# A state update in column tiles of 32 instead of 64, with every engine's order listed anew

## The chip, the cores and the metric

The kernel runs on one core of a Trainium2 chip. The time is the device time of one execution in microseconds (us). The core's engines are TensorE (PE in the rows; PEld is its weight load), VectorE (DVE), ScalarE (ACT), GpSimd (POOL) and SyncE (SP), which issues the DMAs.

## The reference

For 4 batches, 8 heads, 768 steps and 48 features there is a linear recurrence with a complex decay, and behind it a gated layer with a convolution of three taps over the steps:

```python
mag = np.sqrt(a_re * a_re + a_im * a_im)
scale = np.minimum(mag, 0.999) / (mag + 1e-06)
a_re_n, a_im_n = (a_re * scale, a_im * scale)
for t in range(S):
    ar, ai = (a_re_n[:, :, t, :, None], a_im_n[:, :, t, :, None])
    new_re = ar * S_re - ai * S_im
    new_im = ar * S_im + ai * S_re
    kv = np.einsum('bhd,bhe->bhde', k[:, :, t], v[:, :, t])
    S_re, S_im = (new_re + kv, new_im)
    y[:, :, t] = np.einsum('bhd,bhde->bhe', q[:, :, t], S_re)
...
h = np.maximum(x @ w_in, 0.0)          # x: heads side by side, 384 wide; h: 1024 wide
conv_out += conv_w[k][None, None, :] * hp[:, k:k + S, :]
gate = 1.0 / (1.0 + np.exp(-conv_out))
return (h * gate @ w_out)
```

## The kernel before

The steps are cut into chunks of 128, six to a batch, 24 in all, and into 12 segments of two chunks. A segment's decays are turned into running logarithms and angles (`a_pre`, `a_log`, `a_trig`, `c_pre`), then into factors for q and k (`c_exp`, `c_post`); VectorE and ScalarE do this. L553 multiplies k (then q) by the factors into `qkc`, L557 writes that to DRAM (`qk_d`), and L559 reads it back in another layout as `stk`, with 96 rows per head (48 features, real and imaginary).

For a chunk, `c_chunk` turns the 6 blocks of k back to steps by features (transposes, L572), copies them out as `kn` (L573, ScalarE), and adds k times v to a state that stays in PSUM: this is the state update, L579. L586 copies the state to `s_sb`. Then `attention` computes the scores of the chunk (L612, column tiles of 64, 96 rows), masks them (L627), and adds to one PSUM tile, by L636, state by query ("state-by-query", 128 moving columns) and p by v ("p v", 64 moving columns), both in column tiles of 32. `in_turn` writes these so that the four column tiles follow one another: a matmul of tile 0, one of tile 1, of tile 2, of tile 3, and round again. L662 and L663 split the result into two parts for the layer behind.

The layer runs in 10 units of 256 or 384 steps. `moe_front` (L718) multiplies by `w_in`, then relu (L722) and the convolution (L723, L725); `moe_back` has the gate (L413, L737, L743, L746), the product with `w_out` (L753), and the output (L760, L763). These matmuls use the whole array. Weights are unpacked at the start by VectorE, ScalarE and TensorE (L338 to L341, L376 to L383).

The state has 96 rows per head and `kn` 96 columns. Before the change L579 covers them by two column tiles of 64: rows 0 to 63 and 64 to 127. The second takes 32 columns of the next head along (for the last head, 96 columns of zeros that L322 sets once). So one chunk has 8 heads x 2 = 16 matmuls of 64 weight columns and 48 moving columns. An f32 matmul has two records in the trace here (two passes), so a chunk shows 32. Five chunks of a batch's six have an update: 20 in all, 640 records.

The order on each engine is written out by hand. `groups` numbers the program's instructions as they are written (matmuls that follow one another with the same operand and job share a number), `ORDER` lists the numbers for each engine, and `in_order` ties each instruction to the one listed ahead of it:

```python
for eng, line in ORDER.items():
    ...
            for i in row:
                if last is not None:
                    tc.add_manual_dep(i, last.name, ...)
                last = i
```

In the old list the 20 updates have the numbers 178, 184, 240, 246, 389, 595, 601, 767, 773, 961, 1103, 1109, 1240, 1246, 1435, 1577, 1583, 1714, 1720 and 1894. The constants of the convolution are the numbers 36 (its DMA, L346) and 37 to 46 (VectorE, L338 to L357); 19 is the first segment's load of a (L443), 20 its square (L458), 21 the sum behind that (L459), 22 its logarithm (L413).

Of the kernel before, what the change touches and what calls it, by code (L numbers as in the profile page):

```python
# [12 lines left out]
F32 = mybir.dt.float32  # L13
# [7 lines left out]
B, H, S, D = 4, 8, 768, 48  # L21
# [25 lines left out]
QC = 2  # L47
TB = 3
# [21 lines left out]
DSEG = [0] * 12  # L70
# [89 lines left out]
    "DVE": [37, 38, 39, 40, 21, 41, 112, 42, 48, 113, 43, 49, 56, 46, 50, 64, 45, 114, 24, 27, 25, 57, 28, 29, 30,  # L160
# [113 lines left out]
def linear_attention_moe_kernel(ctx: ExitStack, tc: tile.TileContext, a, qk, v, w_in, conv_w, w_out, out):  # L274
    nc = tc.nc

    const = ctx.enter_context(tc.tile_pool(name="const", bufs=1))
# [117 lines left out]
    st = {}  # L395
# [144 lines left out]
    def c_post(p):  # L540
        seg_time(p, OP)
        b, j, m = segs[p]
# [22 lines left out]
    def c_chunk(c, kv, stk, vt):  # L565
        b, j = divmod(c, NC)
        if j < NC - 1:
# [6 lines left out]
            if j == 0:  # L574
                st["sps", b] = psS.tile([128, H, D], F32, name="s_ps")
# [460 lines left out]
```

## Time and profile before

| | |
|---|---|
| median of 3 runs | 393.89 us (392.82 to 394.5) |
| the profiled execution | 393.71 us |
| its span, first to last instruction | 391.9 us |
| mean granted TensorE clock | 0.971 |
| TensorE, VectorE, ScalarE busy | 340.1, 346.8, 336.0 us |

The time of an execution holds a little more than the span (1.8 us here). Busy time is the union of an engine's instructions; a matmul's row also holds the time that it takes to pass through the array, so matmuls overlap, and what a matmul occupies is read from one start to the next.

### The profile page before, as it was taken

The page shows a single profiled execution, that of the slowest core. Times are in us where ns is not written, and L with a number is a line of the kernel's source. Part 1 is how long each engine was busy: PE and PEld are TensorE (multiplying, and loading weights), DVE is VectorE, ACT ScalarE, POOL GpSimd, SP SyncE. Part 2 cuts the span into 40 slices and gives each one's busy share as a digit, 9 for nine tenths or more (in the row PEclk, how much of TensorE's full clock was granted, in tenths as well). Part 3 has the DMA queues.
Part 4 walks back from the last instruction along what each step waited for, and adds up shares of the span by engine and source line. Part 5 has one row for each costly group of instructions (what it writes and reads, how often), then busy time and mean ns, then how long its engine had stood idle before and what let it go on. Part 6 is the DMA issues. An engine that isn't in the chain of part 4 may idle for free.

```text
span 391.9 us, 11311 instructions
## 1 busy us (share of the span) xinstructions
PE 340.1 (87%) x4834; PEld 318.4 (81%) x4834; DVE 346.8 (89%) x567; ACT 336.0 (86%) x555; POOL 5.7 (1%) x38
## 2 busy tenths in 40 slices
PE   0307178899999999999999999999997999999993
PEld 0105147799999998999999999999996999999992
DVE  3999999999999999899999989999998877569680
ACT  5999999999999999899999999999996965354561
POOL 4000000000000000000000000000000000000000
PEclk9999666999999999999999999999999999999999
DMA  7999979895986648794947937939939529101011
GB/s 279 339 336 325 279 256 299 302 243 174 298 236 264 182 104 288 245 267 164 263 170 246 257 110 286 244 96 343 264 129 263 200 82 252 33 22 44 0 42 51
DMA packets 33420, 81.07 MB, mean 207 GB/s; under 512 B 2128, under 2 KB 23632, under 8 KB 31824
## 3 DMA queue, kind: packets, MB, share of 16 engines
q1 hardware_dynamic: 33360, 80.25, 65.2%
q8 instruction: 40, 0.66, 0.7%
q14 instruction: 20, 0.16, 0.1%
HBM read 56.65 MB, written 23.59 MB: 205 GB/s over the span
## 4 chain that ended last, share of the span: by engine, by line
PE 78%; ACT 12%; DVE 6%; issue 2%; DMA 1%; DVEq 0%; ACTq 0%
PE h_ps L718 27%; PE o L753 27%; PE ps L636 9%; PE ps L612 8%; PE s_ps L579 4%; PE ps L572 3%; ACT L265 3%; ACT w_t L458 1%; ACT x_t L413 1%; DVE qkc_t L553 1%; ACT w_t L413 1%; DMA a_t<-in_a 1%; ACT e_t L413 1%; ACT zz_t L413 1%; ACT wi L376 1%
## 5 line engine op out<-in xcount | busy, mean ns | idle before, releaser
L718 PE MATMUL h_ps<-x,wi 128*128 128x258 f32 (+1 forms) x720 | 121.0, 307 | 0.0
L753 PE MATMUL o<-wo,hg 128*128 128x384 f32 x576 | 120.6, 341 | 0.1
L718 PEld LDWEIGHTS h_ps<-x,wi 128*128 128x128 f32 x720 | 109.2, 189 | 1.0 <-ACT h_t L722 0.2
L753 PEld LDWEIGHTS o<-wo,hg 128*128 128x128 f32 x576 | 98.5, 188 | 2.2 <-issue 0.5
L265 ACT ACT_TABLE_LOAD x45 | 57.7, 1283 | 0.8
L612 PE MATMUL ps<-stk 96*64 96x128 f32 (+1 forms) x768 | 41.7, 260 | 8.8 <-DMA stk<-qkd 8.3
L413 ACT ACTIVATE g_t<-g_t,cw 128x256 f32<-128x256 f32 (+1 forms) x80 | 42.1, 547 | 8.0 <-DVE g_t L725 7.5
L612 PEld LDWEIGHTS ps<-stk 96*64 96x64 f32 x768 | 37.1, 144 | 14.0 <-ACT zz_t L525 8.5
L723 DVE SCALAR_TENSOR_TENSOR g_t<-h_t,cw 128x256 f32<-128x256 f32 (+1 forms) x80 | 41.3, 532 | 4.6 <-ACT h_t L722 4.3
L722 ACT ACTIVATE h_t<-h_ps 128x258 f32<-128x258 f32 (+1 forms) x80 | 33.2, 424 | 13.8 <-PE h_ps L718 13.7
L553 DVE TENSOR_TENSOR qkc_t<-e_t,zz_t 128x1536 f32<-128x1536 f32 x24 | 41.9, 1751 | 0.5 <-ACT zz_t L413 0.5
L725 DVE SCALAR_TENSOR_TENSOR g_t<-h_t,cw,g_t 128x256 f32<-128x256 f32 (+1 forms) x80 | 41.3, 533 | 0.8
L737 DVE SCALAR_TENSOR_TENSOR g_t<-g_t,h_t 128x512 f32<-128x512 f32 (+1 forms) x40 | 31.6, 792 | 5.3 <-ACT g_t L413 5.3
L746 DVE TENSOR_TENSOR hg<-g_t,hg 128x512 fp32r<-128x512 f32 (+1 forms) x40 | 31.5, 792 | 4.8 <-ACT hg L743 4.7
L743 ACT ACTIVATE hg<-g_t 128x512 fp32r<-128x512 f32 (+1 forms) x40 | 28.6, 715 | 8.1 <-DVE g_t L737 5.0
L627 DVE TENSOR_TENSOR p_t<-ps,mask 128x384 f32<-128x384 f32 x48 | 26.4, 552 | 5.8 <-PE ps L612 4.8
L636 PE MATMUL ps<-p_t,v_t 128*32 128x64 f32 x1344 | 24.6, 222 | 4.9 <-DVE p_t L627 2.5
L572 PE MATMUL ps<-ident,qkc_t 128*128 128x128 f32 x120 | 18.5, 289 | 11.5 <-DVE qkc_t L553 10.2
L636 PEld LDWEIGHTS ps<-p_t,v_t 128*32 128x32 f32 x1344 | 22.4, 112 | 6.4 <-issue 3.2
L572 PEld LDWEIGHTS ps<-ident,qkc_t 128*128 128x128 f32 x120 | 14.6, 148 | 14.2 <-DVE qkc_t L553 11.1
L579 PE MATMUL s_ps<-v_t,kn 128*64 128x48 f32 x640 | 24.0, 231 | 2.1 <-ACT kn L573 2.1
L579 PEld LDWEIGHTS s_ps<-v_t,kn 128*64 128x64 f32 x640 | 22.0, 147 | 4.6 <-ACT kn L573 3.6
(91 smaller groups left out, 446.1 us busy)
## 6 DMA issues: line engine op xcount, KB each, us to landing
qkd<-qkc_t SPq DMA_DIRECT2D x24, 768.0 KB, 4.0
stk<-qkd SPq DMA_DIRECT2D x24, 768.0 KB, 7.8
v_t<-in_v SPq DMA_DIRECT2D x12, 1024.0 KB, 7.8
a_t<-in_a SPq DMA_DIRECT2D x12, 768.0 KB, 5.3
qk_t<-in_qk SPq DMA_DIRECT2D x12, 768.0 KB, 5.8
out<-os_t SPq DMA_DIRECT2D x24, 192.0 KB, 3.0
hg<-in_w_out SPq DMA_DIRECT2D x8, 384.0 KB, 5.4
h_t<-in_w_in SPq DMA_DIRECT2D x8, 384.0 KB, 5.8
```

The lines of the kernel that those rows point to most:

```text
L265: row = [nc.scalar.preload_act_table_set(loaded).ins] + row
L413: nc.scalar.activation(out, in_, func=func, **kw)
L553: nc.vector.tensor_tensor(out=qkc, in0=e[:, q:q + 1].broadcast_to([128, 2, NG * w]), in1=zz, op=ALU.mult)
L572: nc.tensor.transpose(tr[:, g - lo], kv[:, g // NG, g % NG], ident)
L579: nc.tensor.matmul(sps[r:r + 64, h], lhsT=kn[:, h * 96 + r:h * 96 + r + 64], rhs=vt[:, j % 2, h // 2, 112 * (h % 2):112 * (h % 2) + D], st ...
L612: nc.tensor.matmul(o, lhsT=kt[:, 2 * i + u, part * HC + r:part * HC + r + TM], rhs=qt[:, 2 * i + u, part * HC:C], start=first, stop=part = ...
L636: nc.tensor.matmul(yp[r0:r0 + 32, q // 4, cols], lhsT=left, rhs=right, start=r0 not in started, stop=stop, tile_position=(0, r0), skip_gro ...
L718: nc.tensor.matmul(hp, lhsT=wi[iw][:, f, kt], rhs=x[ix][:, kt], start=(k == 0), stop=(k == 8))
L722: nc.scalar.activation(h, hp, func=AF.Relu)
L723: nc.vector.scalar_tensor_tensor(out=g, in0=h[:, 0:n], scalar=cw[:, f, 0:1], in1=h[:, 1:n + 1], op0=ALU.mult, op1=ALU.add)
L725: nc.vector.scalar_tensor_tensor(out=g, in0=h[:, 2:n + 2], scalar=cw[:, f, 2:3], in1=g, op0=ALU.mult, op1=ALU.add)
L753: nc.tensor.matmul(ops[t][:min(C, n - t * C)], lhsT=hg[:, k, t * C:min((t + 1) * C, n)], rhs=w[:, fw], start=(f == 0 and i == 0), stop=(f ...
```

## The change

The update goes back to three column tiles of 32 for each head: 8 x 3 = 24 matmuls of 32 weight columns per chunk, the three tiles in turn. `kn` has 8 x 96 columns again and comes from a pool with one buffer; its zero columns and their memset (number 17) are gone, so that all higher numbers of the list stand one lower. The state has 96 rows instead of 128. The write of `qkc` to DRAM is written as two runs of a row instead of one. `DSEG` gets longer. All five lists of the order are new; they hold the same groups as before, the memset left out.

```diff
+KB = 1
...
-DSEG = [0] * 12
+DSEG = [0] * 24
...
-    "PE": [52, 53, 60, 61, 174, 176, 178, 68, 69, 180, 76, 182, 77, 186, 188, 84, 92, 93, 85, 190, 195, 184, 197,
...
-    "DVE": [37, 38, 39, 40, 21, 41, 112, 42, 48, 113, 43, 49, 56, 46, 50, 64, 45, 114, 24, 27, 25, 57, 28, 29, 30,
...
-    "ACT": [20, 22, 23, 26, 115, 159, 34, 33, 51, 2, 59, 204, 54, 161, 206, 163, 31, 207, 210, 164, 166, 167, 121,
...
-    "SP": [19, 36, 111, 47, 55, 63, 165, 32, 203, 117, 123, 71, 79, 227, 216, 87, 129, 340, 169, 95, 135, 172, 170,
...
+    "PE": [51, 59, 52, 67, 68, 60, 75, 76, 173, 175, 179, 177, 181, 183, 185, 187, 83, 84, 189, 194, 91, 92, 196,
...
+    "DVE": [36, 37, 38, 39, 40, 41, 42, 43, 44, 111, 45, 112, 20, 47, 113, 48, 55, 49, 63, 56, 64, 26, 23, 24, 57,
...
+    "ACT": [2, 19, 21, 22, 114, 25, 158, 32, 58, 50, 33, 53, 203, 160, 66, 205, 30, 162, 206, 69, 209, 163, 165, 166,
...
+    "SP": [35, 18, 110, 46, 54, 62, 164, 31, 202, 116, 122, 70, 78, 226, 86, 215, 339, 128, 134, 168, 94, 171, 169,
...
-    kn = const.tile([128, (H + 1) * 96], F32, name="kn")
-    nc.gpsimd.memset(kn[:, H * 96:], 0.0)
...
-            nc.sync.dma_start(qk_d.rearrange("p g t -> p (g t)"), qkc.rearrange("p c x -> p (c x)"))
+            nc.sync.dma_start(qk_d.rearrange("p (c g) t -> p c (g t)", c=2), qkc)
...
-            knv = kn[:, 0:H * 96].rearrange("s (h d c) -> s (h d) c", h=H, c=6)
+            kn = sc.tile([128, H, 96], F32, name="kn", bufs=KB)
+            knv = kn.rearrange("s h (d c) -> s (h d) c", c=6)
...
-                st["sps", b] = psS.tile([128, H, D], F32, name="s_ps")
+                st["sps", b] = psS.tile([96, H, D], F32, name="s_ps")
...
-                for r in range(0, 128, 64):
-                    nc.tensor.matmul(sps[r:r + 64, h], lhsT=kn[:, h * 96 + r:h * 96 + r + 64],
+                for r in range(0, 96, 32):
+                    nc.tensor.matmul(sps[r:r + 32, h], lhsT=kn[:, h, r:r + 32],
...
-                           in_=sps[0:96].rearrange("r (i u) d -> r i u d", u=2))
+                           in_=sps.rearrange("r (i u) d -> r i u d", u=2))
```

Where the updates stand in TensorE's two lists, from the third p v on (the last 16 of the 20): in the old one five between two groups of scores, four between scores and L636, six between the layer's matmuls and transposes, one between scores and L718. In the new one six between scores and L636, three between L636 and scores, six between the layer's matmuls and transposes or other matmuls of the layer, one between L753 and scores. Counting every place behind the third p v where the width of the column tiles changes (32, 64 or the whole array), the old list has 79 and the new one, with the update at 32, has 80. The number of activation table loads that the order of ScalarE asks for is 45 by either list.

## Rows read from the trace of the kernel before

**Rows 1.** The page's first part: the span and the engines' busy time.

```profile
span 391.9 us, 11311 instructions
PE 340.1 (87%) x4834; PEld 318.4 (81%) x4834; DVE 346.8 (89%) x567; ACT 336.0 (86%) x555; POOL 5.7 (1%) x38
```

**Rows 2.** The chain that ended last, by engine and by line.

```profile
PE 78%; ACT 12%; DVE 6%; issue 2%; DMA 1%; DVEq 0%; ACTq 0%
PE h_ps L718 27%; PE o L753 27%; PE ps L636 9%; PE ps L612 8%; PE s_ps L579 4%; PE ps L572 3%; ACT L265 3%; ACT w_t L458 1%; ACT x_t L413 1%; DVE qkc_t L553 1%; ACT w_t L413 1%; DMA a_t<-in_a 1%; ACT e_t L413 1%; ACT zz_t L413 1%; ACT wi L376 1%
```

**Rows 3.** Busy time by stretch (PE, PEld, DVE, ACT, POOL; clock, DMA share, GB/s).

```profile
30.00:50.00 20.00, 9.92 (x77) 7.90 (x79) 20.00 (x39) 19.80 (x28) 0.00 (x0) 0.80 0.99 301
50.00:75.00 25.00, 19.64 (x324) 15.14 (x322) 24.93 (x35) 24.85 (x37) 0.00 (x0) 0.75 0.89 274
75.00:120.00 45.00, 44.61 (x748) 42.68 (x744) 44.45 (x77) 43.43 (x87) 0.34 (x4) 1.00 0.80 240
...
346.50:385.40 38.90, 38.87 (x357) 38.23 (x355) 27.79 (x62) 21.07 (x50) 0.00 (x0) 1.00 0.09 32
```

**Rows 4.** The same from 75 us to the last update: sum of five stretches.

```profile
sum 271.50, PE 267.78 PEld 255.48 DVE 250.32 ACT 244.04 POOL 1.37; mean PE 53.56 PEld 51.10 DVE 50.06 ACT 48.81 POOL 0.27
```

**Rows 5.** Groups of instructions, shapes apart.

```profile
L636 PE MATMUL ps<-p_t,v_t 128*32 128x64 f32 x1344 | 24.6, 222 | 4.9 <-DVE p_t L627 2.5 <-issue 2.4
L579 PE MATMUL s_ps<-v_t,kn 128*64 128x48 f32 x640 | 24.0, 231 | 2.1 <-ACT kn L573 2.1
L636 PE MATMUL ps<-stk,s_sb 96*32 96x128 f32 x640 | 22.8, 283 | 0.8 <-issue 0.6
```

**Rows 6.** Busy time of L579 alone, 75 us to the last update.

```profile
75.00:346.50 271.50, 17.83 (x512) 16.32 (x512) 1.00 0.69 211
```

**Rows 7.** Timeline of TensorE around one update (start, length, group, records).

```profile
93.30 0.89 PE L612 MATMUL ps<-stk 96*64 96x128 f32 x16
94.04 1.14 PE L579 MATMUL s_ps<-v_t,kn 128*64 128x48 f32 x32
95.00 0.85 PE L612 MATMUL ps<-stk 96*64 96x128 f32 x16
95.79 1.08 PE L636 MATMUL ps<-stk,s_sb 96*32 96x128 f32 x32
```

**Rows 8.** Timeline of TensorE: an update ahead of transposes, and a p v.

```profile
117.30 1.14 PE L579 MATMUL s_ps<-v_t,kn 128*64 128x48 f32 x32
118.37 0.77 PE L572 MATMUL ps<-ident,qkc_t 128*128 128x128 f32 x5
...
138.74 0.97 PE L636 MATMUL ps<-p_t,v_t 128*32 128x64 f32 x56
139.63 0.45 PE L753 MATMUL o<-wo,hg 128*128 128x384 f32 x1
```

**Rows 9.** TensorE's waits from 75 to 358 us (total, times, longest).

```profile
PE ps L636 <- issue: 3.0, 2, 2.4
```

**Rows 10.** Timeline of VectorE and ScalarE at the start.

```profile
5.44 0.18 DVE L338 TENSOR_SCALAR ct<-cd 128x24 int32<-128x24 int32 x1 [5.44 <-DMA cd<-in_conv_w]
5.66 0.18 DVE L339 SCALAR_TENSOR_TENSOR ct<-cd,ct 128x24 int32<-128x24 int32 x1
...
6.77 0.96 DVE L459 CUSTOM_DVE_ANT_0 w_t<-w_t 128x768 f32<-128x768 f32 x1 [0.51 <-ACT w_t L458]
...
5.26 1.48 ACT L458 ACTIVATE w_t<-a_t 128x1536 f32<-128x1536 f32 x1 [3.17 <-DMA a_t<-in_a]
8.05 1.48 ACT L413 ACTIVATE w_t<-w_t 128x1536 f32<-128x1536 f32 x1
```

**Rows 11.** DMA packets of the whole run, and two kinds of issue.

```profile
DMA packets 33420, 81.07 MB, mean 207 GB/s; under 512 B 2128, under 2 KB 23632, under 8 KB 31824
qkd<-qkc_t SPq DMA_DIRECT2D x24, 768.0 KB, 4.0
v_t<-in_v SPq DMA_DIRECT2D x12, 1024.0 KB, 7.8
```

More of the change, by code (lines that the diff above doesn't have):

```diff
@@ L105 @@
 ORDER = {
[54 rows of a table removed]
-    "DVE": [37, 38, 39, 40, 21, 41, 112, 42, 48, 113, 43, 49, 56, 46, 50, 64, 45, 114, 24, 27, 25, 57, 28, 29, 30,
[27 rows of a table removed]
-    "ACT": [20, 22, 23, 26, 115, 159, 34, 33, 51, 2, 59, 204, 54, 161, 206, 163, 31, 207, 210, 164, 166, 167, 121,
[25 rows of a table removed]
-    "POOL": [191, 3, 192, 10, 4, 15, 18, 11, 5, 13, 0, 8, 1, 9, 12, 16, 14, 7, 6, 17, 398, 397, 609, 608, 790, 789,
[8 rows of a table removed]
[54 rows of a table added]
+    "DVE": [36, 37, 38, 39, 40, 41, 42, 43, 44, 111, 45, 112, 20, 47, 113, 48, 55, 49, 63, 56, 64, 26, 23, 24, 57,
[27 rows of a table added]
+    "ACT": [2, 19, 21, 22, 114, 25, 158, 32, 58, 50, 33, 53, 203, 160, 66, 205, 30, 162, 206, 69, 209, 163, 165, 166,
[25 rows of a table added]
+    "POOL": [190, 3, 191, 10, 4, 15, 17, 11, 5, 13, 0, 8, 1, 9, 12, 16, 14, 7, 6, 397, 396, 608, 607, 789, 788, 1116,
[8 rows of a table added]
 }
```

224 rows, old and new, of the table ORDER are left out of this document.

## The prediction

> **What bounds the kernel now.** I read the chain of waits first: 78% of the time that ends last is TensorE's, and the state update L579 has 4% of it [rows 2]. That VectorE has more busy time than TensorE over the run [rows 1] misleads, since the stretches differ. Up to 75 us VectorE and ScalarE are full and TensorE is not; from 75 us on TensorE is full, to its last matmul at 385.4 us [rows 3]; behind that come only the last output and its DMA, to the span's end at 391.9 [rows 1]. So an update behind the third p v (16 of the 20) counts in full on the path that sets the end, and the four ahead of it are covered by VectorE's and ScalarE's work: there the same microsecond buys nothing. From 75 us to the last update TensorE is busy 267.78 of 271.5 us, VectorE 250.32, ScalarE 244.04 [rows 4]: the next engine has 17 us less to do than TensorE, so a few us off TensorE do not make another engine the bound over the whole stretch, though between 75 and 120 us VectorE has only 0.55 us to spare [rows 3].
>
> **The update itself.** What a group occupies is read from starts. In a group, records follow one another at (its length - one record's own length) / (records - 1). The update has 32 records in 1.14 us, one lasting 0.231 us: 0.909 / 31 = 29.3 ns each, so 59 ns for two neighbours, one on each column tile [rows 7, 5]. Over the 16 updates it is 17.83 / 16 = 1.114 us a group, 28.5 ns a record, and 32 x 28.5 = 0.91 us occupied [rows 6].
>
> The trace of before has no update in tiles of 32. The nearest rows are L636's, which has tiles of 32 in turn. The p v has 56 records in 0.97 us, one lasting 0.222 us: 13.6 ns each, 55 ns for a round of four tiles, at 64 moving columns [rows 8, 5]. State by query has 32 records in 1.08 us, one lasting 0.283 us: 25.7 ns each, 103 ns a round, at 128 columns [rows 7, 5]. So a round of tiles of 32 is set by the moving columns, at (103 - 55) / 64 = 0.75 ns a column, and at 48 columns it should take 55 - 16 x 0.75 = 43 ns. Is there a floor that keeps it at 55? For tiles of 64 there is one: the scores' 16 records occupy 0.74 us from their start to the update's [rows 7], half of them with 128 columns (4 pairs at about 0.103) and half with 64, which leaves 0.33 for 4 pairs and for the change of tile width at their head, at most 0.08 a pair; the update, with a quarter fewer columns, still takes 0.059. There the columns seem to count no longer, and something of the tile's width does. With half the width, whatever it is should be half: the four tiles' weight loads fit into 55 ns, so three take no more than 41. Both ways say about 42. I take 43: per chunk 8 heads x 2 passes = 16 rounds, 16 x 43 = 0.69 us in place of 0.91, 0.22 us less, and 16 x 0.22 = 3.5 us over the run. Bounds: with no round shorter than the shortest seen, 55 ns, it is 0.88 and the gain 16 x 0.03 = 0.5 us; with 0.75 ns x 48 = 36 ns and nothing else it is 0.58 and the gain 5.3 us.
>
> **Changes of tile width.** An update ahead of scores (64 and 64) holds TensorE 0.96 us until the next start, one ahead of transposes (64 and whole) 1.07 us [rows 7, 8]: 0.11 us for the change. From p v to L753 it is 0.89 us where 0.76 are records: 0.13 us. With tiles of 32 the update no longer fits between scores: the five updates that stand so in the old list would make ten changes of 0.12 us, 1.2 us. The new list moves them next to L636, and in sum 79 changes become 80: +0.1 us. Bounds 0 and +0.5 (a change into narrow tiles may cost more than one out of them).
>
> The Trainium skill states the rule behind this (TensorEngine Tiling, Key Properties): changing the tiling mode drains the array. Rule and rows agree here; by it alone, with the old positions kept, the 3.5 us would shrink by the 1.2 us worked out above.
>
> **Issue.** TensorE gets 256 records and as many weight loads more behind the third p v. In 75 to 358 us it stood still twice, 3.0 us in sum, for nothing but "issue", both times in L636's dense bursts [rows 9], which are nearly all of L636's 1,984 records [rows 5]. At that rate 256 more records bring 256 / 1,984 x 3.0 = +0.4 us; bounds 0 and one more stall of the longest sort, +2.4.
>
> **The start.** In the new list of VectorE the sum L459 is no longer fifth but stands behind all ten operations for the convolution's constants and two for the weights, and the constants' DMA is issued ahead of the load of a. Ten operations at 0.22 us from start to start and two longer ones of the weights (about 0.3 and 0.5 us on the engine), some 2.9 us, from 5.44 us on put L459 at 8.3 instead of 6.77, or a little earlier as its constants arrive earlier; the logarithm L413, at 8.05 now, needs its result [rows 10], 0.9 us later, so some 9.0 to 9.2. That is up to 1.1 us of ScalarE idle at the head of a stretch in which ScalarE is full (19.80 of 20.00) [rows 3]. VectorE loses nothing, the twelve had to be done anyway. I take half, +0.5; bounds 0 and +1.1.
>
> **What costs nothing.** The memset is one short instruction on GpSimd, which is idle 99% of the time and busy 5.7 us in 38 instructions [rows 1], 0.15 us each; without that cover so much would be gained. The write of `qkc` in two runs: the load of v is written in two runs too, and above 8 KB there are 33,420 - 31,824 = 1,596 packets, which are its 12 x 128 and little else [rows 11]: runs that adjoin go as one packet. If not, 24 x 128 more packets of half the size, same bytes, behind a landing of 4.0 us. `kn` from a pool of one buffer waits for the update before it, as the one tile did. L586 reads 96 rows either way. `DSEG` is read for 12 segments. Activation tables: 45 loads by both lists.
>
> **The rest of the new order.** The groups are the same, so each engine's sum is the same. Adding up, each instruction at its duration in the old trace (whose sums are [rows 1]), the work that is listed ahead of each of the 24 splits L663, VectorE's differs by at most 1.5 us between the lists for 23 of them; TensorE's ahead of each L636 by at most 2.3. A local reshuffle, with no stall of its own in sight: 0, bounds -1.5 and +3 (TensorE's 3.0 us of waits [rows 9] once more).
>
> **Sum**, against the profiled 393.71 us: -3.5 + 0.1 + 0.4 + 0.5 = -2.5, 391.2 us. The profiled execution is 0.18 us below the median of the runs, so I predict 391.4.
>
> **Rivals.**
> 1. A price per record. If an update's record costs the same whatever its width, 48 x 28.5 = 1.37 us a chunk, 0.46 more, 16 x 0.46 = +7.4, with the other +1.0 some 402 us. For it: in tiles of 64, moving columns no longer count. Against: 13.6 ns a record in the p v, with the same 128 rows and 32 columns [rows 8]. It decides for slower from (0.91 + 0.06) / 48 = 20 ns a record, with the other terms as above. Chance 0.08.
> The Trainium skill has a rule of that kind (TensorEngine Tiling, Instruction Overhead: about 60 cycles a matmul, so that no tiles should be taken from a dimension already small). By its figure, as an estimate, 25 ns x 48 = 1.2 us a chunk and 4.5 us in all, near 399 us; the 13.6 ns speak against it.
> 2. No round below 55 ns: gain 0.5 us, with the other +1.0 a time of 394.4, same. For it: no shorter round is in the trace. Chance 0.13.
> 3. The gain on TensorE comes true and goes into its waits for VectorE and ScalarE, full as those are up to 75 us, VectorE nearly so up to 120 [rows 3]: 393 to 395. Against it: 17 us to spare in sum [rows 4]. Chance 0.17.
> 4. The new lists cost by themselves: a group that TensorE reaches 2 to 5 us ahead of its data, so that all matmuls behind it wait. In the new list one L663, that of the 22nd chunk, has 4.9 us more of VectorE's work ahead of it, and transposes need the bank that it frees. With the start: 396 to 399. Chance 0.10.
> 5. The new lists gain as well, in the start or in the waits: 387 to 389. Chance 0.06.
>
> **How the numbers follow.** The forecast holds 0.46; its own range is 389 to 392.5, from the bounds of the sum. What a measurement here can tell from no change is 0.5%, 2 us: 391.9 and 395.9. Of the forecast 0.02 falls into "same". Faster 0.44 + 0.06 = 0.50; same 0.13 + 0.17 + 0.02 = 0.32; slower 0.08 + 0.10 = 0.18. The range reaches down to the bound of the update's gain with a little of case 5 (387.5) and up to the end of "same" (396), which leaves out case 1, most of case 4 and half of case 5, 0.2 together.
>
> **What would show it.** L579 with 960 records, groups of 48 lasting about 0.69 + 0.22 = 0.91 us at 14 to 15 ns a record; at 18 ns rival 2 is right, at 25 and more rival 1. Its busy time over the 16 updates falls from 17.8 to some 14.5 us. TensorE's last matmul ends at about 382.9 instead of 385.4. L413's first logarithm starts near 9 us. If L579 is shorter and the end is not, TensorE's idle time from 75 us on has grown from 3.7 us, and its waits name the engine. The prediction is wrong above all if the lists matter more than the update does.

## The result, and the profile after

The changed kernel took 390.36 us, median of 5 runs (388.97 to 390.99), against 394.47 us for the kernel before in the same round (392.82 to 394.58): ratio 0.990, 95% interval 0.987 to 0.993. Predicted were 391.4 us (387.5 to 396.0) and "faster" with 0.50. The profiled execution took 388.97 us.

The first part of the page of the kernel after, beside [rows 1]:

```profile
span 387.2 us, 11941 instructions
...
PE 337.4 (87%) x5154; PEld 313.1 (81%) x5154; DVE 347.5 (90%) x567; ACT 335.2 (87%) x555; POOL 5.6 (1%) x37
```

The update among the groups of instructions, beside [rows 5]:

```profile
L579 PE MATMUL s_ps<-v_t,kn 128*32 128x48 f32 x960 | 18.8, 215 | 6.0 <-ACT kn L573 4.2 <-ACT s_sb L586 1.8
```

And the busy time of L579 alone over the stretch of [rows 6]:

```profile
75.00:346.50 271.50, 14.02 (x768) 12.02 (x768) 0.99 0.68 212
```

L579 has half as many records again as before and takes less time: 14.02 us where it took 17.83. The timeline of TensorE around an update (start, length, group, records), beside [rows 7]:

```profile
93.39 0.88 PE L579 MATMUL s_ps<-v_t,kn 128*32 128x48 f32 x48
94.21 1.56 PE L612 MATMUL ps<-stk 96*64 96x128 f32 x32
95.76 0.43 PE L636 MATMUL ps<-stk,s_sb 96*32 96x128 f32 x8
```

(0.88 - 0.215) / 47 = 14.1 ns a record. The starts in a group lie 7, 7 and 29 ns apart, again and again: a round of three tiles every 43 ns. Before, two tiles took 7 and 51 ns, 58 a round.

TensorE's waits from 75 to 358 us (total, times, longest), beside [rows 9]:

```profile
PE ps L636 <- issue: 2.6, 1, 2.6
PE ps L612 <- DVE x L663: 0.5, 1, 0.5
PE h_ps L718 <- ACT x L387: 0.2, 1, 0.2
```

The timeline of TensorE around the longest of them:

```profile
294.61 0.51 PE L636 MATMUL ps<-p_t,v_t 128*32 128x64 f32 x21
297.68 0.75 PE L636 MATMUL ps<-p_t,v_t 128*32 128x64 f32 x35 [2.56 <-issue]
```

And the busy time of the stretch behind it (PE, PEld, DVE, ACT, POOL; granted clock, DMA share, GB/s):

```profile
298.30:301.70 3.40, 3.40 (x19) 3.34 (x14) 2.30 (x4) 3.23 (x8) 0.00 (x0) 0.55 0.58 163
```

The same around the stop of before:

```profile
299.00:306.00 7.00, 4.62 (x83) 4.33 (x76) 4.72 (x9) 4.39 (x8) 0.00 (x0) 1.00 0.97 286
```

The stop in the middle of a p v is of the same kind as the 2.38 us before. What is new is the clock: behind the stop it is granted at half, 1.2 GHz instead of 2.4, for 3.4 us. The matmuls of L753 start 320 ns apart in that stretch and 174 ns apart behind it, so it costs some 1.6 us. In the profile of before the clock was 1.00 from 299 to 306 us, behind its stop as well.

TensorE's last matmul ended at 381.81 us instead of 385.37, 3.56 us sooner (382.9 was forecast). The other 1.1 us of the 4.7 us of span lie behind it, 0.9 of them in the last output, which landed 2.6 us behind the last matmul instead of 3.5. The gain of 4.7 us in the profiles is more than the 4.1 us between the medians, because the profiled execution was the fastest of the five.

### The profile page after: what moved, and what is told of

Same layout as the page of the kernel before. It is cut to its first block, busy times and chain, and to the rows that moved or that the text cites. A ratio compares the mean times of both kernels' runs of the same rounds, so it can differ in the third digit from the quotient of the medians.

```text
span 387.2 us, 11941 instructions
## 1 busy us (share of the span) xinstructions
PE 337.4 (87%) x5154; PEld 313.1 (81%) x5154; DVE 347.5 (90%) x567; ACT 335.2 (87%) x555; POOL 5.6 (1%) x37
## 2 busy tenths in 40 slices
DMA packets 33422, 81.10 MB, mean 209 GB/s; under 512 B 2128, under 2 KB 23632, under 8 KB 31824
## 4 chain that ended last, share of the span: by engine, by line
PE 49%; ACT 28%; DVE 7%; issue 4%; ACTq 0%
PE o L753 17%; PE h_ps L718 17%; PE ps L636 7%; ACT L266 6%; PE ps L612 4%; ACT w_t L412 2%; ACT g_t L412 2%; ACT zz_t L412 2%; ACT x_t L412 2%; PE ps L572 2%; ACT hg L743 2%; ACT w_t L457 2%; ACT h_t L722 2%; PE s_ps L579 1%; ACT x L662 1%
## 5 line engine op out<-in xcount | busy, mean ns | idle before, releaser
L753 PE MATMUL o<-wo,hg 128*128 128x384 f32 x576 | 120.5, 344 | 0.0
L718 PE MATMUL h_ps<-x,wi 128*128 128x258 f32 (+1 forms) x720 | 119.8, 308 | 0.3 <-ACT x L387 0.2
L718 PEld LDWEIGHTS h_ps<-x,wi 128*128 128x128 f32 x720 | 107.7, 189 | 1.2 <-ACT x L387 0.6
L753 PEld LDWEIGHTS o<-wo,hg 128*128 128x128 f32 x576 | 100.2, 191 | 1.1
L612 PE MATMUL ps<-stk 96*64 96x128 f32 (+1 forms) x768 | 40.2, 258 | 6.1 <-DVE p_t L627 3.7
L612 PEld LDWEIGHTS ps<-stk 96*64 96x64 f32 x768 | 36.3, 142 | 11.1 <-issue 4.3
L412 ACT ACTIVATE g_t<-g_t,cw 128x256 f32<-128x256 f32 (+1 forms) x80 | 42.0, 547 | 3.0 <-DVE g_t L725 3.0
L636 PE MATMUL ps<-p_t,v_t 128*32 128x64 f32 x1344 | 24.6, 223 | 2.6 <-issue 2.6
L572 PE MATMUL ps<-ident,qkc_t 128*128 128x128 f32 x120 | 21.4, 298 | 6.1 <-ACT kn L573 5.3
L378 PE MATMUL h_ps<-g_t,ident 128*128 128x384 f32 x16 | 11.3, 802 | 17.4 <-DVE g_t L340 16.8
L636 PEld LDWEIGHTS ps<-p_t,v_t 128*32 128x32 f32 x1344 | 22.7, 113 | 3.8 <-issue 3.0
L573 ACT COPY kn<-ps 128x512 f32<-128x512 f32 (+1 forms) x40 | 19.6, 498 | 5.3 <-PE ps L572 5.2
L579 PE MATMUL s_ps<-v_t,kn 128*32 128x48 f32 x960 | 18.8, 215 | 6.0 <-ACT kn L573 4.2
```

What stands on the lines that cost most here:

```text
L412: nc.scalar.activation(out, in_, func=func, **kw)
L612: nc.tensor.matmul(o, lhsT=kt[:, 2 * i + u, part * HC + r:part * HC + r + TM], rhs=qt[:, 2 * i + u, part * HC:C], start=first, stop=part = ...
L636: nc.tensor.matmul(yp[r0:r0 + 32, q // 4, cols], lhsT=left, rhs=right, start=r0 not in started, stop=stop, tile_position=(0, r0), skip_gro ...
L718: nc.tensor.matmul(hp, lhsT=wi[iw][:, f, kt], rhs=x[ix][:, kt], start=(k == 0), stop=(k == 8))
L753: nc.tensor.matmul(ops[t][:min(C, n - t * C)], lhsT=hg[:, k, t * C:min((t + 1) * C, n)], rhs=w[:, fw], start=(f == 0 and i == 0), stop=(f ...
```

## The experiments

In kernels whose lists were written out anew (the first four), lines from the lists on stand seven later or so: the update is L586, the scores L619, L636 is L643.

### The new code in the old lists

The kernel after with the lists of before, their numbers moved by one for the memset that is gone.

> The code of the change with the old lists (numbers above 17 one lower). If the update's shorter round makes the gain: groups of 48 records of L579 with a round of 43 ns, some 3.5 us off the 16 updates behind the third p v, and about 1.2 us given back, because five updates stand between scores and now change the tile width twice; 391.5 to 392.5 us. If the new lists make the gain: no faster than 393.5.

Measured: 396.62 us against 393.79, ratio 1.0058 (1.0025 to 1.0092). In the old lists the shorter round made the kernel slower, by 0.6%. The timeline of TensorE around an update between scores:

```profile
214.41 0.89 PE L619 MATMUL ps<-stk 96*64 96x128 f32 x16
215.23 0.88 PE L586 MATMUL s_ps<-v_t,kn 128*32 128x48 f32 x48
216.04 0.89 PE L619 MATMUL ps<-stk 96*64 96x128 f32 x16
216.86 1.07 PE L643 MATMUL ps<-stk,s_sb 96*32 96x128 f32 x29
219.86 0.32 PE L643 MATMUL ps<-stk,s_sb 96*32 96x128 f32 x2 [1.93 <-issue]
```

TensorE's waits from 75 us on:

```profile
PE ps L643 <- issue: 4.5, 2, 2.6
PE ps L619 <- DVE x L670: 1.0, 2, 0.6
PE s_ps L586 <- issue: 0.5, 1, 0.5
```

Two stretches by busy time, with the granted clock behind the five times:

```profile
219.70:223.10 3.40, 3.24 (x63) 3.07 (x63) 0.95 (x3) 1.18 (x3) 0.00 (x0) 0.55 1.11 269
305.00:308.40 3.40, 3.40 (x12) 3.40 (x13) 1.99 (x4) 3.37 (x6) 0.00 (x0) 0.55 1.01 341
```

Two things eat the gain. Between scores, the round's 0.22 us goes into the two changes of tile width: scores, update and scores take 216.86 - 214.41 = 2.45 us, and 95.79 - 93.30 = 2.49 us before [rows 7]. And "issue" has 5.0 us where it had 3.0, with two stretches of half clock behind it, 3.4 us each, which cost some 3.4 us more in all. The second is the larger, and where such stops fall depends on the place in the program, as the experiments with added matmuls below show.

### The old code in the new lists

The kernel before, with the lists of after (numbers moved back, the memset put in).

> The code of before (two tiles of 64 a head) with the new lists (numbers from 17 on one higher, the memset put back). If the update's round makes the gain: L579 at 59 ns a pair again, 0.22 us more a chunk and changes of width at both sides of the updates that stand next to L636, 394 to 395 us. If the new lists make it: 390 to 391.

Measured: 392.70 us against 393.79, ratio 0.998 (0.995 to 1.001), between the two values expected. The longest of TensorE's waits from 75 us on:

```profile
PE ps L644 <- issue: 2.0, 1, 2.0
```

Behind this one stop the clock was at half for 3.4 us. Neither part alone gives the 1%.

### Half of the moving columns

24 instead of 48 columns in the update, in the kernel after and in the kernel before; half of the state is left out.

```
rhs=vt[:, j % 2, h // 2, 112 * (h % 2):112 * (h % 2) + 24]
```

> The changed kernel with 24 of the 48 moving columns in each matmul of L579 (the other half of the state is left out, and L586 copies the 24). If the moving columns set the round of three: about 55 - 40 x 0.75 = 25 ns, 8 to 9 ns a record. If the weight loads set it (three at 14 ns): still 41 to 43 ns, 14 ns a record.

> The kernel of before with 24 of the 48 moving columns in each matmul of L579 (the other half of the state is left out). If something of the width of 64 sets the pair's 59 ns: it stays at 58 to 59. If the columns count there after all: 40 ns or less.

Measured: 385.09 us with tiles of 32, 394.51 us with tiles of 64, one run each. The timeline of the update and what follows it with tiles of 32:

```profile
93.03 0.70 PE L586 MATMUL s_ps<-v_t,kn 128*32 128x24 f32 x48
93.65 1.56 PE L619 MATMUL ps<-stk 96*64 96x128 f32 x32
```

The same with tiles of 64:

```profile
95.16 1.07 PE L586 MATMUL s_ps<-v_t,kn 128*64 128x24 f32 x32
96.07 0.87 PE L619 MATMUL ps<-stk 96*64 96x128 f32 x16
```

From start to start the first occupies 0.62 us where 48 columns took 0.82, a round of 32 ns instead of 43. The second occupies 0.91 us; four of the five such places of before took 0.92 and the one in [rows 7] 0.96. Its round is 58 ns, as with 48 columns: with tiles of 64 it makes no difference whether 24 or 48 columns move, with tiles of 32 it does. So there is the floor that the prediction argued for with tiles of 64, and with tiles of 32 it lies at 32 ns or lower. The 32 ns is neither of the two values expected, 25 and 41 to 43.

### The update not in turn

The kernel after with the two loops of the update exchanged, so that neighbours lie on one tile.

```diff
-            for h in range(H):
-                for r in range(0, 96, 32):
+            for r in range(0, 96, 32):
+                for h in range(H):
```

> The kernel after with the loops of the state update exchanged: all eight heads of one tile of 32 columns, then the next tile, so that no two neighbouring matmuls lie on different tiles but two in 48. Theory A (three tiles run beside each other; a tile alone takes the whole round of 43 ns for each matmul): about 43 ns from start to start, 2.0 us instead of 0.67 us for 48, 16 updates behind 75 us on the path: 20 to 22 us more, 410 to 412 us. Theory B (a matmul costs its own weight load of 14 ns, in turn or not): 390.4 us.

Measured: 407.12 us. The timeline around an update:

```profile
97.67 1.95 PE L579 MATMUL s_ps<-v_t,kn 128*32 128x48 f32 x48
99.55 1.56 PE L612 MATMUL ps<-stk 96*64 96x128 f32 x32
```

Within one tile the starts lie 42 to 43 ns apart, so one matmul alone costs what a round of three in turn costs. Around each of the two changes of tile seven starts lie closer, so that 48 matmuls take 1.74 us from the first start to the last and not the 2.0 us expected. The group occupies 1.88 us, 1.06 more; 16 of them make 17.0 us, and the last matmul came 17.7 us later. Two other differences act against each other here: the third p v began 3.9 us later than in the kernel after, and the stops for "issue" were 0.9 and 0.2 us, with no half clock behind them.

### Where the stops for "issue" come from

The page of the kernel after lists a DMA queue of the kind "instruction" whose packets have 16 KB each (packets, MB, share of 16 engines):

```profile
q8 instruction: 42, 0.69, 0.8%
```

I counted TensorE's records (matmuls and weight loads) ahead of each stop. This is worked out from the records of the traces; some are missing, so the last digit can be off by one. The times are counted from the span's start, as in the views; the expectations below have them 0.3 us less:

```
kernel               stop us, at us     records ahead
before               0.64   155.84      3521 = 13 x 256 + 193
                     2.38   302.02      7617 = 29 x 256 + 193
after                2.56   297.68      8129 = 31 x 256 + 193
new code, old lists  0.50   155.55      3778 = 14 x 256 + 194
                     1.93   219.86      5569 = 21 x 256 + 193
                     2.61   304.25      8130 = 31 x 256 + 194
```

Always 193 or 194 behind a multiple of 256. That fits a program that arrives in packets of 256 instructions, with the stops where two packets meet. Each ended 1.4 to 1.6 us after a packet had landed. To test this I moved the program by matmuls of one column by one, put ahead of the first matmul, while TensorE idles:

```diff
                 rest = room()[:, 0:WP]
+                for _ in range(0 if split[0] else 86): nc.tensor.matmul(rest[0:1, 0:1],
+                    lhsT=ident[:, 0:1], rhs=ident[:, 0:1], start=True, stop=True)
```

> The kernel after, with 86 matmuls of one column by one column ahead of the first matmul, into a part of the accumulator that the next matmul overwrites, at a time when TensorE is idle (the first matmul of the kernel after starts at 10.74 us). They add 172 instructions to TensorE's program (a weight load and a matmul each) and move every later instruction 172 places on. Theory 1 (code arrival): TensorE's program comes by DMA in packets of 16 KB, 256 instructions; the idle time put down to 'issue' falls on every 256th place of the program, at the boundary of two packets, and comes where TensorE uses a packet up in under 4.8 us. In the kernel after one such place is left behind 80 us (2.56 us at 297.38 us, with the half clock for 3.5 us behind it, 1.75 us more); moved by 172 places no boundary lies in a dense stretch. Expected: no idle time over 0.5 us behind 80 us, clock 1.00 throughout, 386.1 us (390.4 less 4.3). Theory 2 (the place in the work): the wait belongs to the p v matmuls at 297 us, whatever their place in the program: 390.4 us, or a little more for the added matmuls.

> As the kernel with 86 added matmuls, with 32 of them: 64 places. Theory 1 (code arrival): now six boundaries fall in dense stretches, and TensorE waits 2.4 to 3.3 us at about 98, 156, 259, 294, 315 and 339 us of the kernel after's timeline (each later by the waits ahead of it), 17.6 us in all instead of 2.6; with 1.75 us of half clock behind each of up to six, 405 to 414 us. Theory 2 (the place in the work): 390.4 us, as the kernel after.

> The new code (three tiles of 32 columns) in the old lists, as in the first experiment (396.6 us), with the 86 added matmuls. Theory 1 (code arrival): its waits of 0.50, 1.93 and 2.61 us and the two stretches of half clock behind them (1.75 us each) go: 388.1 us, so that the shorter round alone is worth about 3 us against the kernel before freed of its waits. Theory 2 (the old lists cost what the round gains, by changes of tile width and waits for other engines): 396.6 us.

> The kernel before with the 86 added matmuls. Theory 1 (code arrival): its waits of 0.64 us at 155.54 and 2.38 us at 301.72 us go; the clock stayed at 1.00 behind them in the profile, so 390.8 us (393.8 less 3.0), a little less where other runs had the half clock there. Theory 2 (the place in the work): 393.8 us.

> The kernel after with 64 added matmuls ahead of the first one. In the two runs with 32 and 86 of them each added matmul turned out as two weight loads and two matmuls in the trace, four places of the program and not two, so they moved the program by 128 and 344 places, and 64 of them move it by 256, one whole packet. Theory 1 (code arrival at every 256th place): the boundaries lie at the same work as in the kernel after, so the wait of about 2.6 us at the p v matmuls of 297 us and the half clock behind it come back, and the waits of the kernel with 32 (0.64 us at 133 us) do not appear: 390.4 us and up to 1 us of later start. Theory 2 (the added matmuls change something else, the clock or the start, and any number of them helps or harms): 387.6 us as with 32, or 393.8 as with 86.

> The kernel before with the 32 added matmuls (128 places) that took the kernel after to 387.6 us. Theory 1 (code arrival): the wait of 2.38 us at 301.72 us leaves its place, and each wait that appears instead begins at another 256th place and ends 1.3 to 1.6 us after a packet of TensorE's program has landed; which boundaries wait can't be told ahead. Whatever they are, the end of TensorE's last matmul less its idle time from 75 us on less half of the time at the half clock stays at the kernel before's 381.4 us (385.07 - 3.72), within 1 us, against 376.1 to 377.5 in the kernel after and its moved versions: 391 to 395 us. Theory 2 (32 added matmuls gain by themselves, by the clock or the start, and the changed update has no part in the 387.6): about 388 us, and 376 to 378 us for that difference.

Measured: after with 32 of them 387.59 us, ratio to before 0.981 (0.977 to 0.986); with 64, 389.35, 0.990 (0.985 to 0.994); with 86, 393.80, 0.996 (0.992 to 0.999). New code in old lists with 86: ratio 1.001 (0.996 to 1.005). Before with 32: 393.99 us, 1.000 (0.997 to 1.003); with 86: 393.66, 0.997 (0.994 to 1.000). So the change is worth almost 2% with 32 added matmuls ahead of both kernels (0.981 against 1.000), 1.0% with none, and nothing that can be told with 86 (0.996 against 0.997). The runs of one kernel spread, with 86 over 391.14 to 397.22 us in the kernel after and over 392.06 to 400.62 in the old lists; the stops below are those of the one profiled execution of each, for the kernel after with 86 one of 396.16 us.

The weight loads of the added matmuls, of after with 32 (least, median, most ns; first and last start):

```profile
L377 PEld LDWEIGHTS h_ps<-ident x64: 80/81/83, 3.4 to 5.0; 128*1 128x1 f32 x64
```

The longest of TensorE's waits there from 75 us on:

```profile
PE ps L636 <- issue: 0.6, 1, 0.6
```

The timeline of after with 64, around its one stop:

```profile
295.12 0.51 PE L636 MATMUL ps<-p_t,v_t 128*32 128x64 f32 x22
298.25 0.75 PE L636 MATMUL ps<-p_t,v_t 128*32 128x64 f32 x34 [2.62 <-issue]
```

Its busy time behind the stop, with the clock at 1.00:

```profile
298.00:301.40 3.40, 3.15 (x50) 3.06 (x51) 2.36 (x5) 2.37 (x6) 0.00 (x0) 1.00 0.80 201
```

TensorE's waits of after with 86:

```profile
PE ps L636 <- issue: 3.1, 3, 2.0
PE ps L572 <- issue: 2.7, 1, 2.7
PE h_ps L718 <- issue: 0.7, 1, 0.7
```

And its longest wait in before with 32:

```profile
PE ps L636 <- issue: 2.2, 1, 2.2
```

32 added matmuls gave 64 loads and 64 matmuls, 128 places, twice what the first expectations counted: each f32 matmul has two records, as the update's have. With that, 64 move the program by one whole packet, and the stop is back at the same p v of the same chunk (2.62 us); with 128 places it is gone, and other stops appear. Over all fourteen traces there are 34 stops over 0.2 us behind 80 us that the waits put down to "issue", and every one lies 193 or 194 behind a multiple of 256 and ends 1.3 to 1.7 us after a packet's landing. The kernel before with 32 shows the same: its stop of 2.38 us is gone, and one of 2.18 us stands at 220.29 us. Theory 2, that the stop belongs to the work, has fallen, and so has the theory that added matmuls gain by themselves.

What theory 1 can't do is tell which boundaries stop. It expected six stops, 17.6 us, with 32 added matmuls, and none with 86; there were two (0.64 and 0.25 us) and six (6.7 us), and with 86 the third split also came 1.6 us later. These two forecasts were made for moves of 64 and 172 places, and the runs made 128 and 344, so by themselves they do not test the rule of 4.8 us. The new code in the old lists lost its stops of 1.93 and 2.61 us as expected, and got others of 0.93, 2.70 and 0.38 us, with 3.4 us of half clock; before with 86 got 0.77 and 1.39 us for its 0.64 and 2.38. All fourteen traces together test it: behind 80 us some 100 packets were used up in under 4.8 us, and 29 of them ended in a stop; of some 380 slower ones 5 did. So a packet that is used up fast is at risk, but the rule does not say which one stops: the fetch of a packet that came late began anywhere from 0.0 to 4.8 us after TensorE entered the packet ahead of it, and what sets that is open.

### Updates moved to their scores

Six updates that stood among the layer's matmuls (388, 766, 1102, 1239, 1576, 1713) moved to the scores of their chunk, with two `kn` buffers and the 32 added matmuls.

```diff
-KB = 1
+KB = 2
...
-        857, 774, 776, 778, 779, 831, 832, 858, 859, 862, 863, 782, 784, 772, 786, 787, 956, 860, 861, 889, 890, 893,
+        774, 776, 766, 778, 779, 831, 832, 858, 859, 862, 863, 782, 784, 772, 786, 787, 956, 860, 861, 889, 890, 893,
```

> The kernel after with 32 added matmuls (387.6 us), two kn buffers, and six of the updates moved in TensorE's list from among the expert matmuls to the scores of their chunk (numbers 388, 766, 1102, 1239, 1576 and 1713), with ScalarE's copies of the state moved to the end of that chunk. Each isolated update costs two changes of tile width and one beside the scores one less: ten changes fewer of some 0.11 to 0.25 us each. Theory A (a change of tile width is paid on the path): 1.1 to 2.5 us less than with 32 matmuls alone, 385.1 to 386.5 us. Theory B (the drained array is covered by the next weight loads, or the later copies of the state make waits): 387.6 us or more. Code boundaries move by 96 places between each old and new position only.

Measured: 401.48 us against 393.57, ratio 1.018 (1.013 to 1.022). The longest of TensorE's waits from 75 us on:

```profile
PE ps L636 <- issue: 5.5, 3, 2.1
PE o L753 <- issue: 4.3, 1, 4.3
PE s_ps L579 <- issue: 2.0, 2, 1.0
```

The longest stop in the timeline:

```profile
229.72 0.48 PE L753 MATMUL o<-wo,hg 128*128 128x384 f32 x1 [4.33 <-issue]
```

Neither theory has what happened; theory B's "or more" holds only in the letter. The move puts 96 instructions more into stretches that were dense already, and TensorE ran out of program at seven boundaries, 12.3 us in all in the profiled execution (402.64 us). What ten changes of width are worth can't be read beside that.

## Why the prediction was right, step by step

To compare the kernels without their stops, I take the end of the last matmul, less TensorE's idle time from 75 us on, less half of the time at the half clock (1.7 us a stretch): the rest. Since the third p v does not begin at the same time in all of them, the last column counts the rest from there. All of it is worked out from the traces:

```
lists  tiles                 end     idle   half clock   rest    third p v   from there
old    64   before           385.37   3.72   0           381.7    76.6       305.0
old    64   before, 32 added 385.76   2.74   3.4         381.3    77.2       304.1
old    64   before, 86 added 385.75   2.76   0           383.0    78.4       304.6
old    32                    388.89   6.33   6.8         379.1    76.9       302.3
old    32   86 added         387.93   5.44   3.4         380.8    78.9       301.9
new    64                    385.20   2.83   3.4         380.7    77.0       303.7
new    32   after            381.81   3.66   3.4         376.4    76.5       300.0
new    32   after, 64 added  380.76   3.67   0           377.1    77.1       300.0
new    32   after, 32 added  379.85   2.08   0           377.8    76.7       301.1
new    32   after, 86 added  388.83   7.64   3.4         379.5    78.1       301.4
```

**The update.** Right, in mechanism and size. Forecast were a round of 43 ns, 14 to 15 ns a record, groups of 0.91 us and 14.5 us of busy time; measured 43 ns, 14.1 ns, 0.88 and 14.02. From the first start to the last a group takes 0.671 us instead of 0.892 on average, 3.6 us over the 16 for the 3.5 predicted. Rivals 1 and 2 (a price per record, no round below 55 ns) are out. The Trainium skill's figure of about 60 cycles a matmul (TensorEngine Tiling (Array Packing), Instruction Overhead), 25 ns by the prediction's estimate, differs from the 14.1 ns here, and the measurement decides. Of the two ways to the 43, the moving columns hold at this size: 55 ns at 64 columns and 43 at 48 make 0.75 ns a column, as forecast. The other, three weight loads in no more than 41 ns, was a bound from above and no value: at 24 columns three fit into 32 ns. That both said about 42 was luck. From 48 to 24 columns a column is worth only (43 - 32) / 24 = 0.46 ns. Whether that is another slope or a floor near 32 ns, about half of the 58 with tiles of 64 as the prediction argued, no run here tells.

**Changes of tile width.** Right. That the old places would cost some 1.2 us shows between scores, where next to nothing was left of the 0.22 us in each of five places, 1.1 us in all. Counted from the third p v, tiles of 32 are worth 2.7 us in the old lists, without added matmuls and with 86 of them, and some 3.7 us in the new ones.

**Issue.** This is the step that failed: "At that rate 256 more records bring 256 / 1,984 x 3.0 = +0.4 us". The stops come by a place in the program and by how late a packet is, not by the record. In the kernel after they were 0.4 us shorter, and the cost came from what the sum had not: 3.4 us of half clock behind the stop, some 1.6 us. In the old lists the same term was +2.0 us and some 3.4 us lost at the half clock, outside the bounds of 0 to 2.4, and it alone turned a gain into a loss. With 86 added matmuls the stops took 6.7 us, 4.6 more than in the kernel before with as many, and nothing was left of the change's gain.

**The start.** The step was right, its price not. The timeline of VectorE at the start of the kernel after, beside [rows 10], and then ScalarE's:

```profile
7.98 0.95 DVE L458 CUSTOM_DVE_ANT_0 w_t<-w_t 128x768 f32<-128x768 f32 x1
```

```profile
8.97 1.49 ACT L412 ACTIVATE w_t<-w_t 128x1536 f32<-128x1536 f32 x1
```

The logarithm (L412 now) starts at 8.97 us, as forecast (9.0 to 9.2). But the first split L663 came 1.05 us sooner than before and the third 0.09 us sooner: by then nothing was left of it. Not +0.5 but 0. What made it up was not taken apart.

**What costs nothing.** Right: 33,422 packets against 33,420, 45 table loads as before.

**The rest of the new order.** Taken as 0 with bounds of -1.5 and +3. Counted from the third p v, the new lists are worth 1.3 us with tiles of 64; with tiles of 32 it is 2.3 us without added matmuls and 0.5 with 86. So rival 5 came true in part. Rival 3 did not: TensorE's idle time from 75 us on is 3.66 us against 3.72. Nor did rival 4: behind the late 22nd split (2.3 us later than before) TensorE did not wait.

In sum, in the two profiles: -5.2 us of work (the update, its places and the lists), no change in idle time, +1.7 us of half clock, 3.56 us at the last matmul where 2.5 were predicted. The forecast was near in part because two errors, the lists' gain and the half clock, have opposite signs, and that is luck. The 5.2 is no constant of the change: counted from the third p v the work falls by 5.0 us without added matmuls, by 3.0 with 32 and by 3.2 with 86 ahead of both kernels, and where the other 2 us come from is open. That added matmuls gain nothing by themselves is shown by the version before with 32 of them, which stays at 393.99 us with a rest of 381.3; that the update carries more than half of the gain, by the 2.7 us that it brings in the old lists. The fastest version here is the kernel after with 32 added matmuls, 387.59 us.

## What to carry to other kernels

Cost narrow matmuls by the round over their column tiles, from the nearest group of the same tile width, and ask which of the weights' width and the moving columns sets it; then ask whether the new width fits its neighbours in the list. When a change adds instructions to an engine's dense stretches, count its program too: a "wait for issue" that falls on a fixed step of the instruction count is late code, and then an edit has to be timed in more than one place of the program, since a few instructions ahead of it shifted the result here by about 1.4% (ratios to before of 0.981 and 0.996). Packing dense groups together to save changes of tile width came with 12.3 us of such stops.

## What the runs showed of the hardware that I had not expected

TensorE's program comes during the run in packets of 16 KB, 256 instructions of 64 bytes, and up to 4.33 us passed in one stop for it. Of the 14 stops of 1.9 us and more behind 80 us, nine came with the half clock for 3.4 us (1.93, 2.05, 2.18, 2.28, 2.56, 2.61, 2.67, 2.70 and 4.33 us of stop), which in two of them (2.18 and 2.67) began before the stop had ended, and five did not (1.97, 2.04, 2.13, 2.38 and 2.62); the length of the stop does not decide it, and what does is open. Column tiles taken in turn overlap: three matmuls on three tiles of 32 take 43 ns, and so does one alone. One matmul of one column in f32 was two loads and two matmuls in the trace, like the update's.
